# A transformer block with a written order: 75 of 168 transfers, and some instructions of three engines, change places

## The chip, the cores and the metric

The kernel runs on one core of one Trainium2 chip. The metric is the device time of one execution in microseconds (us). Before the change it is 240.98 us, the median of three runs (239.5, 240.98 and 241.52).

The core has five engines that run side by side, each through its own list of instructions: TensorE (PE; its weight loads are shown apart as PEld), VectorE (DVE), ScalarE (ACT), GpSimd (POOL) and SyncE (SP), which here only issues DMA transfers.

## The reference

One transformer block with conditioned layer norms, for 2048 tokens of 512 channels, all in bfloat16:

```python
mod = silu(c) @ w_mod                      # six vectors of 512: sa, ca, ga, sb, cb, gb
h   = layernorm(x) * (1 + ca) + sa
q, k, v = split(h @ wqkv)                  # 32 heads of 16 channels
# each token sees 8 positions: itself and 2, 4, ... 14 tokens back; earlier than 0 is masked
attn = softmax(sum_d q * k[pos - 2w] / 4)
o    = sum_w attn * v[pos - 2w]
x   = x + ga * (o @ wo)
h   = layernorm(x) * (1 + cb) + sb
x   = x + gb * ((silu(h @ w1) * (h @ w3)) @ w2)     # 1792 hidden channels
```

## The kernel before

**Tiles and stages.** The tokens are 16 tiles of 128. The first norm and the q, k and v projections go over the groups of tiles 0-1, 2-3, 4-7, 8-11 and 12-15; attention goes over pairs of tiles; the second norm and the feed-forward part (FFN) go over the groups 0-1, 2-3, 4-7, 8-11, 12-13 and 14-15. The FFN of early tiles runs on TensorE while VectorE and the DMA engines work on the attention of later ones. Names below: tile T, line Lxxx of the kernel, and the tile name that the profile shows.

- *Projections*: L691 makes q and k, four matmuls to a group, L711 makes v (`sb_v`), which SyncE stores to `v_scratch_dram`.
- *Logits of a tile*: one VectorE product q times shifted k (L742, `sb_pq`, 128x4096), summed over the channels of a head by small matmuls on TensorE (L752). These use 32-column parts of the array and are called "tiled" here, as are those of L855; all others use the whole array.
- *Softmax of a pair*: VectorE L764, L769, L794, L796, L797 (`sb_attn`) with the exponential on ScalarE (L782). TensorE turns the result over (L807), ScalarE copies it (L811, `sb_al`).
- *Values of a tile*: four DMA loads fetch the eight shifted copies of v from `v_scratch_dram` into `sb_vsh` or `sb_vshx`. VectorE multiplies them by `sb_al` (L827, 128x4096), TensorE sums them (L855), ScalarE copies the sum out of PSUM (L861, `sb_ac`), a DMA transpose makes `sb_ot`.
- *Output projection of a tile*: TensorE L867, four matmuls; VectorE L871 adds x and sums the row.
- *Second norm of a pair*: GpSimd L586 (mean), ScalarE L590 (squares, one for each tile), GpSimd L596, L597, L599 (variance, its power -0.5, bias), ScalarE L601 (normalized tile `sb_xn`, one for each tile). Then a DMA transpose into `sb_h` for each tile, and ScalarE L621 (scale and shift, four to a group); the FFN groups of tiles 0-1 and 2-3 go over TensorE and L644 instead.
- *FFN of a group*: for each of 14 blocks of 128 hidden channels, two groups of four matmuls (L883, with w1 and w3), silu on ScalarE (L889, `sb_sg`), product on VectorE (L892, `sb_hh`); then for each tile two halves of seven matmuls with w2 (L921; for tiles 14 and 15 in column halves, L909), the last addition on VectorE (L931, `sb_o`) and the store.
- *Weights* come in by loads that SyncE issues: w1, w3 and w2 in four parts each (`sb_w`). VectorE folds the gates ga and gb into wo and w2 (L946, L952).

**What sets the order.** The program is first recorded in the order of the code, each operation with what it reads and writes, and numbered (1118 operations). Nothing is planned when it is built. A table, ORDER, lists all the numbers in one sequence; each engine gets its own operations in that sequence and executes them strictly in that order, so an instruction that waits holds up everything behind it on its engine. All DMAs but one are issued by SyncE, 168 of them, in that order too. A second table, SLOTS, gives each value that lives in a pool its buffer: the eight PSUM banks, the buffers for `sb_vsh`, `sb_xn`, `sb_sg`, `sb_hh` and so on. Waits come out of both tables (place and synchronize): an operation waits for what wrote its inputs, and for everybody who used its buffer before it.

```python
for v in o.vals:
    if v.pool is not None and v.pool.last.get(v.slot) is not v:
        before = v.pool.last.get(v.slot)
        if before is not None:
            o.prev.extend(before.users)
        v.pool.last[v.slot] = v
...
for d, true in list(o.deps.items()) + [(d, False) for d in o.prev]:
    if d.dma:
        need[("dma", d.group[0].n)] = d
    elif d.eng != e or (true and e not in ("pe", "sp")):
        ...
```

So a wait on another engine is for one instruction of it, the last that is needed, and a wait on a DMA is for its whole group (the four value loads of a tile are one).

Of the kernel before, what the change touches and what calls it, by code (L numbers as in the profile page):

```python
# [272 lines left out]
def _build(p, A_x, A_wqkv, A_wo, B_w1, B_w3, B_w2, c, w_mod, out):  # L273
# [707 lines left out]
    8, 9, 10, 0, 20, 21, 22, 3, 4, 1, 2, 16, 17, 23, 24, 25, 26, 27, 28, 29, 30, 31, 32, 34, 33, 18, 59, 60, 61, 62, 63, 64, 11,  # L981
    12, 13, 65, 55, 19, 56, 5, 36, 6, 7, 57, 58, 66, 67, 68, 69, 70, 71, 72, 73, 74, 75, 76, 77, 78, 79, 80, 81, 82, 91, 38, 92,
    93, 94, 96, 97, 98, 99, 95, 101, 35, 14, 105, 83, 100, 84, 42, 40, 85, 102, 106, 86, 103, 104, 87, 39, 89, 88, 15, 141, 124,
    119, 120, 143, 142, 144, 145, 90, 146, 147, 148, 107, 173, 171, 174, 108, 172, 109, 110, 111, 181, 179, 114, 115, 175, 176,
    116, 125, 126, 127, 128, 129, 130, 182, 121, 153, 180, 154, 156, 155, 112, 177, 150, 178, 149, 152, 151, 117, 135, 131, 132,
    133, 134, 229, 122, 123, 136, 137, 113, 183, 184, 185, 138, 186, 163, 164, 237, 161, 235, 165, 238, 139, 236, 187, 193, 140,
    166, 227, 228, 189, 239, 194, 195, 188, 41, 196, 197, 198, 190, 167, 331, 230, 332, 159, 287, 168, 240, 241, 242, 231, 232,
    233, 246, 333, 289, 157, 191, 192, 211, 118, 209, 288, 234, 244, 290, 199, 162, 339, 281, 158, 160, 347, 245, 212, 210, 243,
    203, 205, 200, 215, 216, 204, 349, 169, 348, 350, 279, 340, 218, 334, 280, 351, 206, 219, 282, 352, 353, 381, 341, 372, 291,
    292, 293, 342, 207, 294, 221, 354, 355, 250, 249, 362, 247, 369, 224, 213, 336, 248, 359, 361, 214, 201, 360, 257, 258, 283,  # L990
    284, 285, 202, 371, 356, 370, 357, 358, 253, 254, 208, 273, 276, 286, 259, 260, 170, 265, 266, 217, 261, 379, 298, 380, 363,
    364, 222, 277, 365, 220, 382, 373, 374, 43, 37, 375, 295, 255, 274, 263, 297, 296, 267, 223, 256, 264, 301, 411, 413, 270,
# [12 lines left out]
    717, 700, 701, 718, 720, 509, 770, 771, 679, 705, 750, 736, 737, 490, 748, 772, 485, 719, 500, 749, 488, 721, 739, 740, 752,
    741, 507, 766, 767, 769, 489, 779, 768, 751, 754, 753, 486, 501, 773, 774, 778, 775, 776, 780, 777, 781, 782, 491, 785, 758,
    759, 760, 327, 783, 755, 529, 502, 510, 508, 492, 784, 798, 818, 511, 512, 503, 531, 532, 680, 830, 493, 513, 330, 530, 831,
    521, 539, 832, 514, 515, 820, 822, 814, 799, 815, 522, 819, 504, 505, 516, 517, 541, 494, 324, 520, 495, 518, 506, 834, 806,
    786, 807, 496, 761, 836, 794, 833, 823, 835, 677, 821, 838, 858, 808, 859, 681, 533, 534, 559, 519, 523, 535, 809, 837, 540,
    558, 542, 543, 524, 860, 525, 570, 790, 796, 795, 788, 797, 545, 861, 791, 810, 787, 789, 802, 792, 793, 526, 544, 536, 547,  # L1010
    546, 549, 548, 862, 537, 569, 538, 550, 803, 527, 528, 839, 863, 864, 804, 805, 811, 551, 594, 812, 813, 866, 824, 825, 867,
    800, 567, 593, 552, 553, 554, 874, 592, 868, 869, 826, 557, 816, 560, 801, 840, 827, 870, 871, 555, 872, 568, 556, 817, 876,
    841, 865, 854, 875, 561, 873, 846, 877, 828, 571, 842, 595, 881, 562, 572, 829, 577, 563, 584, 855, 879, 578, 579, 564, 573,
    850, 856, 580, 574, 878, 880, 906, 908, 581, 596, 565, 566, 575, 576, 954, 857, 585, 907, 583, 909, 918, 919, 894, 582, 586,
    843, 956, 955, 957, 886, 887, 958, 756, 898, 587, 588, 895, 597, 890, 891, 589, 926, 847, 598, 599, 959, 960, 962, 899, 900,
    901, 927, 961, 848, 590, 910, 600, 591, 601, 1032, 920, 921, 963, 964, 965, 892, 893, 967, 966, 1034, 928, 1033, 1035, 1036,
# [60 lines left out]
```

## Time and profile before

| | |
|---|---|
| median of three runs | 240.98 us |
| the profiled execution's own time | 239.43 us |
| its span (first to last instruction shown) | 237.7 us |
| TensorE busy | 229.7 us, 97% of the span, 1781 matmuls |
| weight loads (beside matmuls) | 136.2 us, 57% |
| VectorE busy | 179.4 us, 75% |
| ScalarE busy | 138.5 us, 58% |
| GpSimd busy | 29.2 us, 12% |
| SyncE's DMA queue (q1), share of the 16 DMA engines' time | 66.9%, 38.56 MB |
| granted TensorE clock | 1.00 |

Times in the rows are microseconds from the start of the span. A row of the timeline gives the start, the duration, the engine, the line, the operation, output and inputs, shapes, how many instructions are taken together (x4), and in brackets how long the engine had been idle before and what ended that. A row of the chain gives start, length and what the end of the program hung on in that time. The shares are means over stages of different kinds: up to about 150 us attention and FFN run side by side, and VectorE and DMA are busy; behind that only FFN is left, and VectorE and ScalarE are half idle.

### The profile page before, as it was taken

To read this page: it belongs to the slowest core of one execution; us is meant where nothing else is said; L and a number is where in the kernel's file an instruction comes from. 1 tells how busy PE (TensorE), PEld (TensorE's weight loads), DVE (VectorE), ACT (ScalarE), POOL (GpSimd) and SP (SyncE) were. 2 spreads that over 40 slices of the span, in tenths; PEclk is the share of its full clock that TensorE was granted. 3 is DMA by queue.
4 is the path that set the end of the run, shared out by engine and by line. 5 is a ranking of instruction groups with operands and counts; after the bars stand their busy time and mean duration, and the time that the engine had idled before them with its cause. 6 is when DMAs were issued, how large, how long until landed. Compare 5 with 4: busy or idle time off the path is not lost.

```text
span 237.7 us, 4535 instructions
## 1 busy us (share of the span) xinstructions
PE 229.7 (97%) x1781; PEld 136.2 (57%) x1806; DVE 179.4 (75%) x279; ACT 138.5 (58%) x267; POOL 29.2 (12%) x66
## 2 busy tenths in 40 slices
PE   7999999999999998999999999999999999999995
PEld 4776454445588674664444444444475457485774
DVE  5699999999999989999999999682654403434433
ACT  2289577999978744985865594837473405040300
POOL 4434100013002000240002520012010000000000
PEclk9999999999999999999999999999999999999999
DMA  6999999999999999897981693642203000000202
GB/s 216 372 337 322 158 237 299 208 269 283 353 200 270 243 249 199 173 260 177 247 234 47 182 234 72 154 132 46 67 19 91 3 0 0 6 19 0 70 0 88
DMA packets 46317, 38.85 MB, mean 163 GB/s; under 512 B 21704, under 2 KB 37080, under 8 KB 46296
## 3 DMA queue, kind: packets, MB, share of 16 engines
q1 hardware_dynamic: 46288, 38.56, 66.9%
q8 instruction: 14, 0.23, 0.4%
q14 instruction: 7, 0.06, 0.1%
q10 hardware_dynamic: 8, 0.00, 0.0%
HBM read 29.62 MB, written 4.21 MB: 142 GB/s over the span
## 4 chain that ended last, share of the span: by engine, by line
PE 74%; DMA 8%; DVE 8%; SPq 4%; ACT 3%; issue 2%; ACTq 0%; DVEq 0%
PE pall L883 38%; PE pall L921 18%; DMA sb_x<-in_A_x_dram 5%; PE pall L867 5%; SPq L124 4%; PE pall L691 4%; DMA sb_vsh<-v_scratch_dram 3%; PE pall L909 3%; PE pall L855 2%; PE pall L752 2%; PE pall L711 2%; DVE sb_vsh L827 2%; DVE sb_pq L742 2%; DVE sb_hh L892 1%; ACT sb_h L621 1%
## 5 line engine op out<-in xcount | busy, mean ns | idle before, releaser
L883 PE MATMUL pall<-sb_h,sb_w 128*128 128x256 bf16 (+1 forms) x664 | 101.9, 307 | 1.8 <-DVE sb_hh L892 0.9
L883 PEld LDWEIGHTS pall<-sb_h,sb_w 128*128 128x128 bf16 x672 | 64.8, 98 | 37.2 <-issue 2.8
L889 ACT ACTIVATE sb_sg<-pall 128x256 bf16<-128x256 f32 (+1 forms) x84 | 35.6, 453 | 54.1 <-PE pall L883 53.0
L892 DVE TENSOR_TENSOR sb_hh<-sb_sg,pall 128x256 bf16<-128x256 bf16 (+1 forms) x84 | 39.9, 505 | 34.8 <-PE pall L883 32.7
L921 PE MATMUL pall<-sb_w,sb_hh 128*128 128x512 bf16 x190 | 44.0, 379 | 0.3
L742 DVE TENSOR_TENSOR sb_pq<-sb_q,sb_kT 128x4096 bf16<-128x4096 bf16 x16 | 36.3, 2282 | 0.0
L921 PEld LDWEIGHTS pall<-sb_w,sb_hh 128*128 128x128 bf16 x196 | 19.0, 98 | 21.6 <-DVE sb_hh L892 0.4
L691 PE MATMUL pall<-sb_h,sb_wqkv 128*128 128x512 bf16 (+1 forms) x154 | 30.2, 335 | 0.5 <-issue 0.2
L827 DVE TENSOR_TENSOR sb_vsh<-sb_vsh,sb_al 128x4096 bf16<-128x4096 bf16 x12 | 27.3, 2287 | 2.1 <-DMA sb_vsh<-v_scratch_dram 2.1
L621 ACT ACTIVATE sb_h<-sb_h,sb_modc 128x512 bf16<-128x512 bf16 (+1 forms) x24 | 16.5, 743 | 10.1 <-DMA sb_h<-sb_xn 10.1
L691 PEld LDWEIGHTS pall<-sb_h,sb_wqkv 128*128 128x128 bf16 x160 | 14.7, 98 | 11.8 <-ACT sb_ac L861 0.4
L931 DVE TENSOR_TENSOR sb_o<-pall,sb_x 128x512 bf16<-128x512 f32 (+1 forms) x18 | 11.1, 625 | 10.5 <-PE pall L921 6.8
L711 PE MATMUL pall<-sb_wqkv,sb_h 128*128 128x512 bf16 x62 | 15.5, 379 | 0.2
L867 PE MATMUL pall<-sb_wo,sb_ot 128*128 128x512 bf16 x61 | 15.3, 379 | 0.3 <-issue 0.2
L586 POOL TENSOR_SCALAR sb_nm<-sb_sx 128x2 f32<-128x2 f32 x8 | 1.7, 218 | 105.2 <-DVE sb_x L871 105.1
L644 ACT ACTIVATE sb_h<-pall,sb_modc 128x256 bf16<-128x256 bf16 (+1 forms) x18 | 9.9, 612 | 7.5 <-DVE sb_modc L509 6.5
L861 ACT ACTIVATE sb_ac<-pall 128x512 bf16<-128x512 f32 x16 | 9.5, 595 | 7.2 <-PE pall L855 7.1
L601 ACT ACTIVATE sb_xn<-sb_x,sb_nb,sb_rs 128x512 bf16<-128x512 bf16 x16 | 12.4, 806 | 0.7 <-POOL sb_nb L599 0.6
L871 DVE SCALAR_TENSOR_TENSOR sb_x<-pall,sb_x 128x512 bf16<-128x512 f32 x16 | 10.9, 686 | 1.5 <-PE pall L867 1.3
L590 ACT ACTIVATE sb_xn<-sb_x,sb_nm 128x512 bf16<-128x512 bf16 x16 | 11.4, 714 | 0.7 <-POOL sb_nm L586 0.7
L721 ACT ACTIVATE sb_v<-pall 128x512 bf16<-128x512 f32 x16 | 9.5, 600 | 2.8 <-PE pall L711 2.8
L555 DVE BATCH_NORM_STATS2 sb_st<-sb_x 128x6 f32<-128x512 bf16 x16 | 10.6, 680 | 0.8 <-DMA sb_x<-in_A_x_dram 0.7
(87 smaller groups left out, 208.3 us busy)
## 6 DMA issues: line engine op xcount, KB each, us to landing
sb_vsh<-v_scratch_dram SPq DMA_DIRECT2D x48, 256.0 KB, 5.5
sb_vshx<-v_scratch_dram SPq DMA_DIRECT2D x16, 256.0 KB, 4.6
sb_w<-in_B_w_dram SPq DMA_DIRECT2D x6, 512.0 KB, 7.9
sb_w<-in_B_w_dram SPq DMA_DIRECT2D x6, 384.0 KB, 5.4
v_scratch_dram<-sb_v SPq DMA_DIRECT2D x16, 128.0 KB, 6.4
out_dram<-sb_o SPq DMA_DIRECT2D x14, 128.0 KB, 1.8
sb_wqkv<-in_A_wqkv_dram SPq DMA_DIRECT2D x6, 256.0 KB, 6.3
sb_x<-in_A_x_dram SPq DMA_DIRECT2D x4, 256.0 KB, 6.4
```

Source lines behind the costliest of these rows:

```text
L590: p.op("act", lambda e, vn=vn, T=T: e.activation(vn.at[:], x_sb[:, T, :], ACT.Square, bias=nm[:, T, :], accum_out=var[:, T, :]), c_act(512 ...
L601: p.op("act", lambda e, vn=vn, T=T: e.activation(vn.at[:], x_sb[:, T, :], ACT.Identity, bias=nb[:, T, :], scale=rs[:, NT + T, :]), c_act(5 ...
L621: return e.activation(vh.at[:, ft, 0:n * P], vh.at[:, ft, 0:n * P], ACT.Identity, bias=modc[:, 8 * which + ft:8 * which + ft + 1], scale=m ...
L691: ins = e.matmul(bank(vp)[:, j * n:(j + 1) * n], wqkv[:, t, col:col + P], vh.at[:, t, 0:n], start=(t == ORDER[0] and j == 0), stop=(t == O ...
L711: ins = e.matmul(bank(vp), vh.at[:, t, tt * P:(tt + 1) * P], wqkv[:, t, 2 * D:3 * D], start=(t == ORDER[0]), stop=(t == ORDER[-1]))
L742: return e.tensor_tensor(vp.at[:], in0, in1, ALU.mult)
L827: return e.tensor_tensor(v_w, v_w, a_w, ALU.mult)
L867: ins = e.matmul(bank(vy), vt.at[:, ft, :], wo[:, ft, :], start=(ft == 0), stop=(ft == KT - 1))
L883: ins = e.matmul(bank(vp)[:, 0:n], wt[:, t, fi * P:(fi + 1) * P], vh.at[:, t, 0:n], start=(t == 0), stop=(t == KT - 1))
L889: p.op("act", lambda e: e.activation(vt.at[:, 0:n], bank(vgp)[:, 0:n], ACT.Silu), c_act(n), k, r=[vgp], w=[vt], table="silu")
L892: p.op("dve", lambda e: e.tensor_tensor(vh_.at[:, 0:n], vt.at[:, 0:n], bank(vup)[:, 0:n], ALU.mult), c_dve(n), k, r=[vt, vup], w=[vh_])
L921: ins = e.matmul(bank(vz), vhh[fi].at[:, tt * P:(tt + 1) * P], w2[:, fi, :], start=(fi == 0), stop=(fi == NF - 1))
```

## The change

Only the two tables change. The operations, their shapes and their numbers are the same; so are the opening of ORDER (up to about 28 us in the trace of before) and all of GpSimd's order. Place by place, 75 of SyncE's 168 transfers and 22 to 31 operations each of TensorE (of 384), VectorE (of 263) and ScalarE (of 241) change places; counted against the longest sequence that the two orders have in common it is 69, 30, 21 and 26. SLOTS is new from the first value behind the opening on, since buffers are handed on in another sequence.

An extract of the diff; the numbers are operations:

```diff
 ORDER = [
...
-    284, 285, 202, 371, 356, 370, 357, 358, 253, 254, 208, 273, 276, 286, 259, 260, 170, 265, 266, 217, 261, 379, 298, 380, 363,
-    364, 222, 277, 365, 220, 382, 373, 374, 43, 37, 375, 295, 255, 274, 263, 297, 296, 267, 223, 256, 264, 301, 411, 413, 270,
+    359, 357, 358, 253, 371, 254, 208, 370, 286, 273, 276, 259, 297, 220, 260, 265, 266, 261, 379, 170, 296, 380, 363, 364, 222, 37,
+    277, 365, 43, 382, 255, 274, 373, 374, 375, 263, 267, 256, 264, 411, 413, 270, 298, 295, 301, 278, 49, 268, 335, 412, 262, 300,
...
-    521, 539, 832, 514, 515, 820, 822, 814, 799, 815, 522, 819, 504, 505, 516, 517, 541, 494, 324, 520, 495, 518, 506, 834, 806,
-    786, 807, 496, 761, 836, 794, 833, 823, 835, 677, 821, 838, 858, 808, 859, 681, 533, 534, 559, 519, 523, 535, 809, 837, 540,
-    558, 542, 543, 524, 860, 525, 570, 790, 796, 795, 788, 797, 545, 861, 791, 810, 787, 789, 802, 792, 793, 526, 544, 536, 547,
-    546, 549, 548, 862, 537, 569, 538, 550, 803, 527, 528, 839, 863, 864, 804, 805, 811, 551, 594, 812, 813, 866, 824, 825, 867,
+    516, 517, 541, 518, 504, 505, 506, 494, 495, 520, 834, 806, 786, 807, 496, 836, 794, 833, 593, 823, 531, 835, 821, 838, 858,
+    808, 859, 860, 861, 522, 862, 863, 864, 677, 533, 324, 534, 535, 865, 519, 523, 809, 595, 837, 540, 560, 542, 543, 524, 525,
+    790, 796, 795, 788, 797, 545, 791, 810, 557, 787, 789, 802, 792, 793, 544, 594, 547, 546, 536, 549, 548, 550, 803, 570, 761,
+    839, 804, 805, 811, 551, 812, 526, 527, 528, 537, 538, 568, 813, 866, 824, 558, 825, 867, 800, 552, 553, 554, 868, 869, 826,
...
 ]
 SLOTS = [
...
```

Where single operations went (place in ORDER before, then after):

| operations | what they are | before | after |
|---|---|---|---|
| 374 | TensorE: sum of the values of tile 1 (L855) | 301 | 306 |
| 255 | TensorE: a group of L691 | 306 | 303 |
| 391, 392, 393, 394 | SyncE: the four value loads of tile 2 | 395, 377, 391, 389 | 333, 371, 358, 345 |
| 401, 404 | SyncE: the first value loads of tile 3 | 363, 349 | 370, 365 |
| 226 | SyncE: store of v, tile 7 | 435 | 397 |
| 44, 45, 46, 47 | SyncE: loads of w3 part 0, w1 and w3 part 1, w1 part 2 | 342, 418, 426, 464 | 379, 387, 402, 407 |
| 50, 51, 52 | SyncE: loads of w3 part 3, w2 parts 0 and 1 | 448, 437, 434 | 378, 440, 411 |
| 453, 517 | TensorE: L807 of tiles 6 and 10 | 488, 709 | 492, 706 |
| 768, 769, 776, 777 | ScalarE: L601 of tiles 4, 5, 6, 7 | 651, 648, 661, 663 | 636, 633, 654, 656 |
| 859, 860 | ScalarE: L590 of tiles 8 and 9 | 733, 748 | 731, 732 |
| 861, 862, 863 | GpSimd: L596, L597, L599 of tiles 8 and 9 | 757, 772, 781 | 733, 735, 736 |
| 864, 865 | ScalarE: L601 of tiles 8 and 9 | 782, 820 | 737, 743 |
| 535, 525 | ScalarE: copies of the sums of tiles 11 and 10 (L861) | 740, 749 | 742, 754 |
| 847 | TensorE: the second L921 half of tile 5 | 886 | 851 |
| 565, 575 | TensorE: output projections of tiles 12 and 13 (L867) | 854, 856 | 864, 867 |
| 566, 576 | VectorE: their residuals (L871) | 855, 857 | 865, 868 |
| 960, 961 | ScalarE: L601 of tiles 12 and 13 | 890, 896 | 876, 875 |
| 887 | ScalarE: a silu (L889) of the FFN of tiles 8 to 11 | 874 | 880 |

In the new ORDER, then, the four value loads of tile 2 start ahead of several stores of v and weight loads; ScalarE runs both L590 and the first L601 of tiles 8 and 9 ahead of the copy of tile 11 (before, that L601 stood some 40 places behind it); and the output projections of tiles 12 and 13 stand behind one more half of L921 and two more groups of L883. At the very end the last column halves of L921 and L909 with their stores are in another sequence.

115 rows, old and new, of tables (ORDER, SLOTS) are left out of this document.

## The prediction

> **What bounds the kernel now.** I read the table by stage first, then the chain that ended last, then the timeline where a wait stands. The table's columns are the stretch, its length, the busy time of TensorE (PE), its weight loads (PEld), VectorE (DVE), ScalarE (ACT) and GpSimd (POOL), the granted clock, the share of the DMA engines, GB/s.
>
> ```profile
> core 0: us, PE busy (x) PEld busy (x) DVE busy (x) ACT busy (x) POOL busy (x), PEclk, DMA share, GB/s
> 27.00:64.00 37.00, 36.33 (x341) 18.32 (x335) 36.41 (x42) 33.07 (x62) 3.84 (x6) 1.00 1.06 264
> 64.00:88.00 24.00, 23.89 (x233) 18.42 (x236) 22.32 (x33) 18.05 (x40) 1.31 (x4) 1.00 1.12 246
> 88.00:100.00 12.00, 10.72 (x79) 5.97 (x79) 11.86 (x21) 7.49 (x14) 0.62 (x4) 1.00 0.94 186
> 100.00:127.00 27.00, 26.68 (x186) 13.90 (x189) 26.81 (x30) 17.93 (x31) 3.50 (x7) 1.00 0.87 211
> ...
> 174.00:235.00 61.00, 60.74 (x414) 40.66 (x416) 23.33 (x49) 17.30 (x41) 1.06 (x3) 1.00 0.09 27
> ```
>
> TensorE is full at clock 1.00, except at 88 to 100, where 1.28 us are missing. VectorE is as full up to 127, the DMA engines up to 88. Full could still mean slow, so the pace is checked in the chain (start, us, what), with two of its other links:
>
> ```profile
> 52.65 7.64 DMA sb_vsh<-v_scratch_dram
> 60.31 2.29 DVE sb_vsh L827
> ...
> 137.05 6.04 PE pall L883 x28
> ```
>
> 28 matmuls of 512 columns in 6.04 us are 0.216 us each, and the other long links run at that pace. So the work of TensorE, which the change leaves as it is, is a floor. A new order can gain only the few waits that are there, and it loses wherever TensorE comes to stand. One L867, L883 or L711 group of four such matmuls is 0.86 us, one half of L921 (seven) 1.51 us.
>
> **The change part by part.** Times below are on the clock of this trace; a shift that all engines share is added at the end.
>
> **1. The value loads of tiles 2 and 3 come earlier.** These are the SyncE issues around them (48.92 and 50.10 are stores of v; the other issues up to 53.29 are loads):
>
> ```profile
> 44.59 0.57 SPq L124 DMA_DIRECT2D v_scratch_dram<-sb_v  x1
> 45.20 1.20 SPq L124 DMA_TRANSPOSE sb_ot<-sb_ac  x1
> 46.45 0.59 SPq L124 DMA_DIRECT2D sb_vsh<-v_scratch_dram  x1
> 47.08 0.59 SPq L124 DMA_DIRECT2D sb_w<-in_B_w_dram  x1
> ...
> 87.14 2.29 DVE L827 TENSOR_TENSOR sb_vsh<-sb_vsh,sb_al 128x4096 bf16<-128x4096 bf16 x1 [1.04 <-DMA sb_vsh<-v_scratch_dram]
> ...
> 89.82 0.77 PEld L883 LDWEIGHTS pall<-sb_h,sb_w 128*128 128x128 bf16 x8 [1.15 <-DVE sb_hh L892]
> ```
>
> In the new order the second sb_ot transpose follows the first with no store between. It waits for the copy of tile 1, which TensorE now makes one L691 group later, so it is issued at about 44.1 and the first load at 45.3, not 46.45. The store of v11 and a 512 KB weight load no longer stand among the eight loads. The engines' share is 1.06 to 1.12, so the transfers are served one behind the other, and those up to the values of tile 7 are nearly the same set. What starts 1.1 us sooner ends about 1.1 us sooner, if the queue never runs dry. SyncE stands from about 54 to 57.7 for the copy of v7 at its new place, but some eight transfers of 256 to 512 KB are then outstanding; at 246 GB/s one takes 1.07 us or more, so they last. The 1.04 us before the product at 87.14 goes. TensorE's wait at 89.82 came from the L892 groups behind that product, so it goes as well. What is late next is the value load of tile 6, which lands just behind that of tile 7 and shifts with it. From there VectorE and TensorE are both sooner by **1.0 us**. Ends: 0 (the queue runs dry) and 1.3 (the 0.25 us between 60.06 and 60.31, where the chain hangs on the load, counted too).
>
> **2. Small moves.** The rows: TensorE behind a tiled stretch, TensorE at 64, a copy on ScalarE and its reader.
>
> ```profile
> 162.41 1.41 PEld L883 LDWEIGHTS pall<-sb_h,sb_w 128*128 128x128 bf16 x8 [0.42 <-issue]
> ...
> 63.94 0.82 PE L883 MATMUL pall<-sb_h,sb_w 128*128 128x256 bf16 x6 [0.23 <-DVE sb_attn L797]
> ...
> 104.18 0.60 ACT L811 ACTIVATE sb_al<-pall 128x512 bf16<-128x512 bf16 x1 [0.41 <-PE pall L807]
> ...
> 107.49 2.28 DVE L827 TENSOR_TENSOR sb_vshx<-sb_vshx,sb_al 128x4096 bf16<-128x4096 bf16 x1
> ```
>
> Tile 1's sum (L855) is parted from the L752 group: 15 stretches of tiled matmuls for 14, at 0.42 us each by the first row. Half of it is covered at 64, where TensorE waited 0.23 for VectorE anyway. The transposes of attention of tiles 6 and 10 (L807) move ahead of a group, to where L797 ends just then: 0.05 to 0.15 us each. Sum **+0.3 us**, ends 0 and 0.8. The reorder of L601 for tiles 4 to 7 puts ScalarE's L811 of 104.18 up to 2.5 us later; it ended at 104.78 and its reader on VectorE starts at 107.49, 2.7 later, so I take 0. The new order of the weight loads costs 0 too: the one whose lead shrinks most, the second part of w3, should land near 63 and is read at 68.5.
>
> **3. ScalarE: L601 of tile 8 ahead of the copy of tile 11.**
>
> ```profile
> 125.39 2.29 DVE L827 TENSOR_TENSOR sb_vshx<-sb_vshx,sb_al 128x4096 bf16<-128x4096 bf16 x1
> 127.59 1.28 DVE L892 TENSOR_TENSOR sb_hh<-sb_sg,pall 128x512 bf16<-128x512 bf16 x2
> 128.79 2.28 DVE L742 TENSOR_TENSOR sb_pq<-sb_q,sb_kT 128x4096 bf16<-128x4096 bf16 x1
> 131.59 2.28 DVE L742 TENSOR_TENSOR sb_pq<-sb_q,sb_kT 128x4096 bf16<-128x4096 bf16 x1
> ...
> 124.22 0.73 ACT L590 ACTIVATE sb_xn<-sb_x,sb_nm 128x512 bf16<-128x512 bf16 x1
> 127.65 0.60 ACT L861 ACTIVATE sb_ac<-pall 128x512 bf16<-128x512 f32 x1 [2.60 <-PE pall L855]
> 128.14 0.71 ACT L590 ACTIVATE sb_xn<-sb_x,sb_nm 128x512 bf16<-128x512 bf16 x1
> 129.00 0.60 ACT L861 ACTIVATE sb_ac<-pall 128x512 bf16<-128x512 f32 x1
> ...
> 129.03 2.10 POOL L596 TENSOR_SCALAR sb_rs<-sb_var 128x2 f32<-128x2 f32 x1 [6.64 <-ACT sb_xn L590]
> 131.21 0.70 POOL L597 TENSOR_TENSOR sb_rs<-sb_rs,sb_cst 128x2 f32<-128x2 f32 x1
> 131.99 1.94 POOL L599 TENSOR_TENSOR sb_nb<-sb_nm,sb_rs 128x2 f32<-128x2 f32 x1
> ...
> 129.10 3.19 PE L883 MATMUL pall<-sb_h,sb_w 128*128 128x512 bf16 x14 [0.16 <-ACT sb_xn L590]
> ```
>
> Now the copies of tiles 11 and 10 (L861) go out at 127.65 and 129.00, and the matmul at 129.10 writes into the bank that the first of them frees. In the new order ScalarE has both L590 first (124.22, 124.95), then L601 of tile 8, then that copy. L601 needs GpSimd's L596, L597 and L599. L596 would start at 125.70, in the middle of the L827 at 125.39, and the trace shows that it doesn't get through: at 129.03 it took 2.10 us and ended 0.06 after the L742 of 128.79. So: L596 ends 127.74, L597 127.82 to 128.52, L599 128.60 to 128.80, L601 starts at 128.87. ScalarE's next instruction starts 0.70 later: the copy runs 129.57 to 130.17, and the matmul of 129.10 starts at about 130.3. All behind it on ScalarE waits too: the other L601, the copy of tile 10, three L889. Their readers on TensorE follow 0.9 us apart and find them done. **+1.2 us**, which nothing later gives back on an engine that is full. Ends: 0 and +3.5; the first if L596 is through before 125.39, the second if L599 (128.60) comes to lie behind L742 (128.79) and waits 2.3 us more, as L599 did at 131.99.
>
> **4. The output projections of tiles 12 and 13 later, with L601 ahead of L889.**
>
> ```profile
> 156.57 0.69 DVE L871 SCALAR_TENSOR_TENSOR sb_x<-pall,sb_x 128x512 bf16<-128x512 f32 x1
> 157.36 0.22 POOL L586 TENSOR_SCALAR sb_nm<-sb_sx 128x2 f32<-128x2 f32 x1 [15.43 <-DVE sb_x L871]
> 159.52 1.55 POOL L596 TENSOR_SCALAR sb_rs<-sb_var 128x2 f32<-128x2 f32 x1 [1.94 <-ACT sb_xn L590]
> 166.12 0.83 ACT L601 ACTIVATE sb_xn<-sb_x,sb_nb,sb_rs 128x512 bf16<-128x512 bf16 x1
> 166.63 2.58 SPq L124 DMA_TRANSPOSE sb_h<-sb_xn  x2
> 170.40 2.07 ACT L621 ACTIVATE sb_h<-sb_h,sb_modc 128x256 bf16<-128x256 bf16 x4 [3.46 <-DMA sb_h<-sb_xn]
> 173.00 3.04 PEld L883 LDWEIGHTS pall<-sb_h,sb_w 128*128 128x128 bf16 x27
> ```
>
> TensorE does one L921 half and two L883 groups ahead of these L867: 1.51 + 2 x 0.86 = 3.2 us. The L871 of tile 13 moves from 156.57 to about 159.8, ends 160.5, and VectorE goes straight into L827 of tile 14 (160.4 to 162.7). GpSimd's L586, which took 0.22 at 157.36, meets it as L596 met one at 159.52 (1.55 us, to its end): done 162.7. Then two L590 (1.4), L596 to L599 (1.2), two L601 (1.5) end at 167.1, against 166.95 now: what ScalarE no longer queues ahead of them pays for the late start. Two transposes (2.6) and their landing (1.2) give 170.9; L621 now stands behind one more L889, and ends at 173.2 instead of 172.47. The first L883 of the group of tiles 12 and 13, that of 173.00, must wait for it until 173.3. TensorE wants them sooner than now: two L867 (1.72) have gone behind them and one L883 group (0.86) ahead, so at 172.15. **+1.1 us.** Ends: 0 (L586 gets in before L827, 2.1 us sooner) and +1.9 (the last L889 is late as well). Behind it the L867 of tiles 14 and 15 run about 12 us later, but their L883 come at 209, 20 us on: 0.
>
> **5. The end.** The last four L921 groups are permuted, not shortened; the last store hangs on the last of them as before: 0, at most +0.3.
>
> Sum: -1.0 + 0.3 + 1.2 + 1.1 = **+1.6 us**. The profiled execution took 239.43 us, 237.7 of it span; it becomes 241.0, or 0.7% more. That execution is 1.55 below the median of 240.98 (239.5 to 241.52), so on the median's scale I say **242.6**.
>
> **The rivals.**
> *A, clearly slower: GpSimd loses at 128.6.* One mechanism: the third small GpSimd instruction starts 0.19 us before L742 in my sum; if it starts after, it waits for the whole L742, and ScalarE and TensorE with it. +2.3, so +3.9: 244.9. For it: 0.19 us is less than the scatter of these steps. Against it:
>
> ```profile
> 100.75 0.20 POOL L599 TENSOR_TENSOR sb_nb<-sb_nm,sb_rs 128x2 f32<-128x2 f32 x1
> 100.83 2.28 DVE L742 TENSOR_TENSOR sb_pq<-sb_q,sb_kT 128x4096 bf16<-128x4096 bf16 x1
> ```
>
> With a start 0.08 before L742, L599 took its plain 0.20. The Trainium skill says so too ("SBUF — State Buffer", Who interferes with whom): a two-input VectorE instruction and a GpSimd read share a port pair, and whoever issues first has it for the whole instruction. By that rule the 0.19 us decide alone, and A would be out; the trace agrees here, but by the rule L742 would also have lost 0.12 us at 100.83, and its 2.28 is that of all L742.
>
> *B, the lead of part 1 is lost.* SyncE stands three times between 54 and 64.4 (v7, copies of tiles 3 and 2); if the DMA engines run dry there, the values of tile 7 land at 87.1 as now: +2.6, 243.6.
>
> *C, not slower: GpSimd first.* The same shared order, the other way: if L590 of tile 9 is done 0.3 us sooner than 125.66 relative to L827, L596 is through before it, and L601 costs 0.4 instead of 1.2; if L586 gets in ahead of the L827 of tile 14, part 4 is 0. -1.0 + 0.3 + 0.4 = -0.3: 240.7.
>
> **How the numbers follow.** Forecast 0.46 (241.5 to 244.0), A 0.20 (to 246), B 0.12, C 0.18 (down to 239.7, with part 1 at its better end), and 0.04 for something unseen, such as a weight load too late. About 1% (2.4 us) is what a measurement of this kernel tells from no change. Slower by more than that: A, half of B, the top of the forecast and the unseen, 0.37. Faster: the tail of C, 0.03. The range runs from the end of C to that of A: 239.8 to 246.0.
>
> **What would show it.** Part 1: no idle time of VectorE before L827 near 86, and TensorE 1 us ahead at 93. Part 3: ScalarE idle some 3 us before an L601 near 128, and an idle time of TensorE's L883 put down to L861. Part 4: a POOL L586 of about 2 us near 162, and L883 waiting for L621 near 172. The prediction is wrong if TensorE's busy time from 125 to 135 is as full as now, or if idle time appears in stages where I put none.

## The result and the profile after

Over 18 runs each, the changed kernel takes 242.74 us (median; 241.38 to 245.99) and the one before 239.87 (238.44 to 242.93). The ratio is **1.0144, 95% interval 1.0120 to 1.0167**: slower, by 2.9 us by the medians and 3.4 by the ratio. Executions slower than the fastest of the same kernel by over 1.5% are left out of the ratio, but not of the medians and ranges. The forecast was 242.6, and the time lies inside its range, with slower by over 1% at 0.37. That the number was hit so closely is luck: two errors cancel. The time before, taken from three runs as 240.98, is 1.1 lower by 18 runs, and the change costs about twice the +1.6 us of the sum.

The profiled execution of the changed kernel took 242.68 us, 240.9 of it span, against 239.43 and 237.7. Its table by stage, with the columns of the one shown of before (stretch, length, busy time of TensorE, weight loads, VectorE, ScalarE, GpSimd, clock, DMA share, GB/s):

```profile
64.00:88.00 24.00, 24.00 (x250) 17.96 (x243) 23.36 (x34) 18.39 (x40) 1.31 (x4) 1.00 1.14 251
88.00:100.00 12.00, 11.26 (x84) 6.29 (x83) 11.37 (x19) 7.89 (x16) 0.41 (x2) 1.00 0.90 201
100.00:127.00 27.00, 26.94 (x189) 14.25 (x187) 26.81 (x32) 18.54 (x33) 2.82 (x8) 1.00 0.77 198
174.00:235.00 61.00, 60.47 (x405) 39.41 (x404) 22.46 (x49) 19.92 (x48) 1.31 (x4) 1.00 0.10 22
```

TensorE misses less between 88 and 100 than before (0.74 us for 1.28), so something was gained there; but a stretch by the clock holds other work in each kernel. So I compared when TensorE has the same amount of work behind it in both traces, after minus before (where both orders have done the same operations, this is the start of the same one):

| at (us, before) | 24 | 84 | 93 | 96 | 109 | 127 | 132 | 144 | 150 | 168 | 174 | 234 |
|---|---|---|---|---|---|---|---|---|---|---|---|---|
| after minus before | +1.01 | +0.98 | -0.16 | +0.62 | +0.59 | +0.72 | +1.85 | +1.98 | +1.98 | +2.56 | +3.27 | +3.27 |

It starts 1.0 behind in the opening, where both orders are the same; gains 1.1 by 93 and loses 0.8 of it at 95; loses 1.1 near 130, and 1.3 between 150 and 174. Nothing changes behind. The opening is not the change's doing: both orders are the same there, and from the second load on (the first weights of the conditioning, 7.70 us for 6.71) the loads land about 1.0 us later in this execution. VectorE's wait for a load of x shows it, before and then after:

```profile
12.46 0.69 DVE L555 BATCH_NORM_STATS2 sb_st<-sb_x 128x6 f32<-128x512 bf16 x1 [0.71 <-DMA sb_x<-in_A_x_dram]
```

```profile
13.45 1.29 DVE L555 BATCH_NORM_STATS2 sb_st<-sb_x 128x6 f32<-128x512 bf16 x2 [0.94 <-DMA sb_x<-in_A_x_dram]
```

In the 13 other traces of this study (two of them with another warm-up) TensorE is 0.1 to 3.2 us behind the trace of before at 24 us, with the same order up to there. Now the three places, in the timeline of the changed kernel. At the front, VectorE's product of tile 7 has lost its wait, and an L867 has one:

```profile
87.00 2.28 DVE L827 TENSOR_TENSOR sb_vsh<-sb_vsh,sb_al 128x4096 bf16<-128x4096 bf16 x1
...
96.09 0.61 PE L867 MATMUL pall<-sb_wo,sb_ot 128*128 128x512 bf16 x2 [0.64 <-DMA sb_ot<-sb_ac]
```

Near 130, the chain of part 3: GpSimd, VectorE's L742, ScalarE, TensorE.

```profile
126.55 1.72 POOL L596 TENSOR_SCALAR sb_rs<-sb_var 128x2 f32<-128x2 f32 x1 [3.62 <-ACT sb_xn L590]
128.36 0.71 POOL L597 TENSOR_TENSOR sb_rs<-sb_rs,sb_cst 128x2 f32<-128x2 f32 x1
129.14 0.20 POOL L599 TENSOR_TENSOR sb_nb<-sb_nm,sb_rs 128x2 f32<-128x2 f32 x1
...
129.33 2.29 DVE L742 TENSOR_TENSOR sb_pq<-sb_q,sb_kT 128x4096 bf16<-128x4096 bf16 x1
...
129.38 0.81 ACT L601 ACTIVATE sb_xn<-sb_x,sb_nb,sb_rs 128x512 bf16<-128x512 bf16 x1 [2.90 <-POOL sb_nb L599]
130.10 0.58 ACT L861 ACTIVATE sb_ac<-pall 128x512 bf16<-128x512 f32 x1
...
130.73 1.47 PE L883 MATMUL pall<-sb_h,sb_w 128*128 128x512 bf16 x6 [1.10 <-ACT sb_ac L861]
```

Between 162 and 176, that of part 4:

```profile
161.76 0.69 DVE L871 SCALAR_TENSOR_TENSOR sb_x<-pall,sb_x 128x512 bf16<-128x512 f32 x1 [0.16 <-PE pall L867]
162.37 2.29 DVE L827 TENSOR_TENSOR sb_vsh<-sb_vsh,sb_al 128x4096 bf16<-128x4096 bf16 x1
...
162.54 2.19 POOL L586 TENSOR_SCALAR sb_nm<-sb_sx 128x2 f32<-128x2 f32 x1 [17.98 <-DVE sb_x L871]
...
164.77 0.72 ACT L590 ACTIVATE sb_xn<-sb_x,sb_nm 128x512 bf16<-128x512 bf16 x1 [5.01 <-POOL sb_nm L586]
167.67 1.52 ACT L601 ACTIVATE sb_xn<-sb_x,sb_nb,sb_rs 128x512 bf16<-128x512 bf16 x2 [1.37 <-POOL sb_nb L599]
172.99 0.60 ACT L889 ACTIVATE sb_sg<-pall 128x512 bf16<-128x512 f32 x1 [0.40 <-DVE sb_hh L892]
173.48 2.07 ACT L621 ACTIVATE sb_h<-sb_h,sb_modc 128x256 bf16<-128x256 bf16 x4
...
169.72 4.86 PEld L883 LDWEIGHTS pall<-sb_h,sb_w 128*128 128x128 bf16 x24 [0.94 <-ACT sb_sg L889]
175.60 2.41 PEld L883 LDWEIGHTS pall<-sb_h,sb_w 128*128 128x128 bf16 x23 [1.02 <-ACT sb_h L621]
```

ScalarE stands idle for 5.01 us behind L586, and for 1.37 more; seven L889 and copies queue behind it, and TensorE waits twice.

### The profile page after: what moved, and what is told of

The parts are those of the page before. It is cut to its first block, busy times and chain, and to the rows that moved or that the text cites. A ratio compares the mean times of both kernels' runs of the same rounds, so it can differ in the third digit from the quotient of the medians.

```text
span 240.9 us, 4562 instructions
## 1 busy us (share of the span) xinstructions
PE 233.2 (97%) x1806; PEld 136.3 (57%) x1806; DVE 179.5 (75%) x279; ACT 138.1 (57%) x267; POOL 26.5 (11%) x66
## 4 chain that ended last, share of the span: by engine, by line
PE 67%; DMA 9%; ACT 8%; DVE 6%; POOL 4%; issue 2%; SPq 2%; ACTq 0%; DVEq 0%
PE pall L883 31%; PE pall L921 13%; PE pall L691 7%; PE pall L867 5%; DMA sb_ot<-sb_ac 5%; PE pall L711 4%; DMA sb_x<-in_A_x_dram 3%; PE pall L909 3%; DVE sb_st L555 2%; PE pall L752 2%; SPq L124 2%; ACT sb_xn L601 2%; ACT sb_h L621 2%; DVE sb_pq L742 2%; ACT sb_sg L889 2%
## 5 line engine op out<-in xcount | busy, mean ns | idle before, releaser
L883 PE MATMUL pall<-sb_h,sb_w 128*128 128x256 bf16 (+1 forms) x672 | 102.4, 308 | 2.1 <-ACT sb_ac L861 1.1
L883 PEld LDWEIGHTS pall<-sb_h,sb_w 128*128 128x128 bf16 x672 | 64.8, 98 | 38.1 <-ACT sb_ac L861 1.6
L892 DVE TENSOR_TENSOR sb_hh<-sb_sg,pall 128x256 bf16<-128x256 bf16 (+1 forms) x84 | 39.6, 506 | 32.8 <-PE pall L883 24.6
L889 ACT ACTIVATE sb_sg<-pall 128x256 bf16<-128x256 f32 (+1 forms) x84 | 35.6, 456 | 45.9 <-PE pall L883 44.4
L921 PE MATMUL pall<-sb_w,sb_hh 128*128 128x512 bf16 x196 | 44.8, 379 | 0.0
L742 DVE TENSOR_TENSOR sb_pq<-sb_q,sb_kT 128x4096 bf16<-128x4096 bf16 x16 | 36.4, 2285 | 0.0
L691 PE MATMUL pall<-sb_h,sb_wqkv 128*128 128x512 bf16 (+1 forms) x160 | 31.2, 337 | 0.4 <-DVE sb_st L555 0.4
L921 PEld LDWEIGHTS pall<-sb_w,sb_hh 128*128 128x128 bf16 x196 | 18.9, 98 | 22.1 <-issue 0.4
L827 DVE TENSOR_TENSOR sb_vsh<-sb_vsh,sb_al 128x4096 bf16<-128x4096 bf16 x13 | 29.4, 2288 | 0.1
L931 DVE TENSOR_TENSOR sb_o<-pall,sb_x 128x512 bf16<-128x512 f32 (+1 forms) x18 | 11.2, 630 | 16.2 <-PE pall L921 12.4
L691 PEld LDWEIGHTS pall<-sb_h,sb_wqkv 128*128 128x128 bf16 x160 | 14.6, 97 | 12.0 <-issue 0.9
L621 ACT ACTIVATE sb_h<-sb_h,sb_modc 128x512 bf16<-128x512 bf16 (+1 forms) x24 | 16.2, 746 | 6.2 <-DMA sb_h<-sb_xn 6.2
L590 ACT ACTIVATE sb_xn<-sb_x,sb_nm 128x512 bf16<-128x512 bf16 x16 | 11.4, 717 | 11.1 <-POOL sb_nm L586 11.1
L586 POOL TENSOR_SCALAR sb_nm<-sb_sx 128x2 f32<-128x2 f32 x8 | 3.7, 465 | 122.3 <-DVE sb_x L871 122.3
L601 ACT ACTIVATE sb_xn<-sb_x,sb_nb,sb_rs 128x512 bf16<-128x512 bf16 x16 | 12.5, 809 | 7.3 <-POOL sb_nb L599 7.1
L867 PE MATMUL pall<-sb_wo,sb_ot 128*128 128x512 bf16 x64 | 15.5, 379 | 0.6 <-DMA sb_ot<-sb_ac 0.6
L711 PE MATMUL pall<-sb_wqkv,sb_h 128*128 128x512 bf16 x64 | 16.0, 379 | 0.0
L871 DVE SCALAR_TENSOR_TENSOR sb_x<-pall,sb_x 128x512 bf16<-128x512 f32 x16 | 10.9, 685 | 3.7 <-PE pall L867 3.6
L861 ACT ACTIVATE sb_ac<-pall 128x512 bf16<-128x512 f32 x16 | 9.2, 594 | 6.1 <-PE pall L855 3.7
## 6 DMA issues: line engine op xcount, KB each, us to landing
v_scratch_dram<-sb_v SPq DMA_DIRECT2D x16, 128.0 KB, 5.0
out_dram<-sb_o SPq DMA_DIRECT2D x14, 128.0 KB, 1.8
```

Of the source, the lines that this page charges most:

```text
L601: p.op("act", lambda e, vn=vn, T=T: e.activation(vn.at[:], x_sb[:, T, :], ACT.Identity, bias=nb[:, T, :], scale=rs[:, NT + T, :]), c_act(5 ...
L621: return e.activation(vh.at[:, ft, 0:n * P], vh.at[:, ft, 0:n * P], ACT.Identity, bias=modc[:, 8 * which + ft:8 * which + ft + 1], scale=m ...
L691: ins = e.matmul(bank(vp)[:, j * n:(j + 1) * n], wqkv[:, t, col:col + P], vh.at[:, t, 0:n], start=(t == ORDER[0] and j == 0), stop=(t == O ...
L711: ins = e.matmul(bank(vp), vh.at[:, t, tt * P:(tt + 1) * P], wqkv[:, t, 2 * D:3 * D], start=(t == ORDER[0]), stop=(t == ORDER[-1]))
L742: return e.tensor_tensor(vp.at[:], in0, in1, ALU.mult)
L827: return e.tensor_tensor(v_w, v_w, a_w, ALU.mult)
```

## The experiments

ORDER can be cut: where both orders have done the same (or all but the same) operations, one can be followed up to there and the other behind, with the buffers renamed at the seam. (Compared place by place, the lists of SyncE, TensorE, VectorE and ScalarE differ in 118, 100, 51 and 76 places, since one moved operation shifts those behind it; the 75 and the 22 to 31 given ahead come from one matching of the lists.)

### One stage at a time

```diff
 # x1_front: the new order for its first 594 places (96 us), the old one behind
-ORDER = old
+ORDER = new[:594] + [n for n in old if n not in new[:594]]
 # x2_mid: old, new from place 704 to 832 (118 to 148 us), old
 # x3_tail: old[:832], then new
```

> The new order up to the second transpose group of tiles 4 to 7 (about 96 us, where both orders have done the same operations), the old order behind it: parts 1 and 2 alone. By the prediction: -1.0 + 0.3 = -0.7 us against before (ratio 0.997), VectorE without its wait of 1.04 near 87. What the trace of the changed kernel suggests instead: TensorE is 1.2 us ahead at 93, and gives 0.8 back at 95 to 96, where L867 waits for the transpose of tile 7, so -0.4 us (0.998). Rival B (lead lost): 0 (1.000), and the wait of VectorE near 87 is there.

> The old order up to about 118 us, the new one from there to about 148, the old one behind: part 3 alone. By the prediction +1.2 us (ratio 1.005): GpSimd's L596 ends with the L827 that it meets, L601 starts 3 us after its L590, and L883 waits some 1.2 us longer for the copy of tile 11. Rival A: +3.5 (1.015), L599 of 2.3 us or more. Rival C: 0 to +0.4 (1.001).

> The old order up to about 148 us, the new one behind: parts 4 and 5 alone. By the prediction +1.1 us (ratio 1.005), TensorE waiting once, at the first L883 of tiles 12 and 13. By the trace of the changed kernel two waits, 0.6 at an L883 for ScalarE's L889 and 0.7 at that first L883: +1.3 (1.0055). Rival C: 0 (1.000). If the end (part 5) costs what part 4 doesn't explain, up to +0.3 more, behind 225 us.

Measured, as ratios to before, 12 runs each against 35 of before (median 239.32):

| new order in | ratio (95%) | us |
|---|---|---|
| front | 1.0018 (0.9981 to 1.0055) | +0.4 |
| middle | 1.0051 (1.0015 to 1.0086) | +1.2 |
| tail | 1.0046 (1.0008 to 1.0084) | +1.1 |

Parts 3 and 4 cost what the prediction said. The sum is +2.7 us; the whole, 1.0144, makes +3.4 with an interval from +2.9, so that up to some half us stays without a place, within the intervals of the three. What is wrong is the front: its interval, -0.5 to +1.3 us, leaves out the gain of 0.7 that was forecast. Its trace does show the gain (TensorE 0.27 behind before at 36 us, 0.38 ahead at 109), and in its timeline VectorE has no wait ahead of L827:

```profile
86.25 2.28 DVE L827 TENSOR_TENSOR sb_vsh<-sb_vsh,sb_al 128x4096 bf16<-128x4096 bf16 x1
95.12 1.04 PE L867 MATMUL pall<-sb_wo,sb_ot 128*128 128x512 bf16 x4 [0.47 <-DMA sb_ot<-sb_ac]
```

### The front: is it the transfers, and why does an L867 wait?

```diff
 # x4_front_load: x1_front, one load of values of tile 8 (489) behind the transpose of tile 6 (462)
-... 489, ... 462, ...
+... 462, 489, ...
 # x13_sp_front: the old order on all engines but SyncE; SyncE has that of x1_front
```

> The first experiment of this set with one load of values of tile 8 issued behind the transpose of tile 6 in place of between the transposes of tiles 7 and 6. If that load, issued 0.04 us behind the transpose of tile 7, is what delays its landing by 2 us: L867 at 95 no longer waits 0.6, and the time falls by 0.6 to 0.8 us against the first experiment, to -1.0 to -1.2 against before (ratio 0.995). If the weight load issued before it is the cause: no change against the first experiment (within 0.1 us).

> Before, with SyncE's new order up to 96 us alone: the other engines keep their old orders. If the transfers are what moves the time at the front: as the first experiment, VectorE's wait near 87 gone and the ratio to before within 0.3% of it (0.999 to 1.004). The transpose of tile 7: if the order of the transfers makes it late, it lands 2.9 us behind the end of its issue here too; if the fetch of instructions does, it lands 1.1 us behind, as the fetch keeps its place among TensorE's instructions, and the time is 0.5 to 0.8 us below the first experiment (0.997).

The load of tile 8 isn't it: 1.0017 (0.9986 to 1.0048), the transpose still 2.8 us behind the end of its issue. But this trace, with the front of x1_front up to 92 us, has the wait that the change was to remove:

```profile
87.36 2.29 DVE L827 TENSOR_TENSOR sb_vsh<-sb_vsh,sb_al 128x4096 bf16<-128x4096 bf16 x1 [1.03 <-DMA sb_vsh<-v_scratch_dram]
```

And kernels with the old front have it shorter: 0.30 us in x9_silu_first (below), none in x12_before_warm.

```profile
86.41 2.29 DVE L827 TENSOR_TENSOR sb_vsh<-sb_vsh,sb_al 128x4096 bf16<-128x4096 bf16 x1 [0.30 <-DMA sb_vsh<-v_scratch_dram]
```

So the landing of these values scatters by more than the lead. In traces whose openings differ by at most 1 us, they land at 85.4 to 87.3 in the new order (six traces, mean 86.4) and at 85.4 to 87.4 in the old one (six, mean 86.7); the wait is 0, 0, 0, 0.28, 0.85 and 1.03 in the new, and 0, 0.30, 0.42, 1.04, 1.05 and 1.15 in the old. The means differ by 0.3 us, not 1.0, and that is less than the scatter of either set. Two things go with the scatter, neither of them tested. In ten of the 14 traces, of both orders, the DMA queue moves next to no data for 0.9 to 1.5 us between 67.8 and 72 us, with loads outstanding (69.2 to 70.5 in the trace of before); a 16 KB packet that fetches instructions starts 0.5 to 1.3 us before the standstill. The third of the four loads lands at 84.3 to 87.3 in these ten, and at 82.9 to 83.4 in the four others. The fourth load, which ends the wait, follows 1.0 to 1.9 us later in the ten, and 2.2 to 3.5 in the four.

x13_sp_front, SyncE's order alone, is at 1.0028 (1.0003 to 1.0053): slower by itself, by an interval that hardly clears 1. TensorE leads by 1.2 us at 90, and then loses 1.0 of it:

```profile
90.89 3.65 SPq L124 DMA_TRANSPOSE sb_ot<-sb_ac  x2
95.24 1.04 PE L867 MATMUL pall<-sb_wo,sb_ot 128*128 128x512 bf16 x4 [0.97 <-DMA sb_ot<-sb_ac]
```

The DMA view of the same trace from 91.6 to 95.6 us, in slices of 0.1 us:

```profile
GB/s 1 0 0 0 15 161 287 287 287 228 46 164 1 0 0 0 0 0 0 0 0 0 0 0 0 0 18 169 282 289 289 207 49 8 0 0 1 0 0 0
q8 instruction: 1, 0.02, 2.0%
```

The transpose of tile 7 ends its issue at 92.09 and moves its data at 92.0 to 92.7, at once, with the queue empty. Yet it counts as landed at 95.19, 3.1 us behind. What comes at 92.8, at the end of its data, is one 16 KB packet of q8, the queue that fetches instructions. Over the 14 traces, the two transposes of tiles 7 and 6 land 1.1 to 1.7 us behind the end of their issue in 19 cases, and 2.2 to 3.1 in nine; in these nine, and in none of the others, such a fetch begins between 0.25 us before and 0.91 after that end. (The bounds are read off these same 28 cases.) In the old order it falls on the transpose of tile 6 or on none (8 of 8), in the new one on that of tile 7, which TensorE wants at once (5 of 5; 0.4 to 1.0 us of wait; the sixth, with another warm-up, follows below). The packet takes about 1 us, so the time of the packet alone doesn't make the 2 us of delay. In x13_sp_front 30 of the 32 four-byte packets that close the transpose are through at 92.90; the last two end at 94.11, just as the fetch's packet does (92.79 to 94.10), and the landing follows 1.1 us later.

By its expectation, the 3.1 us of x13_sp_front speak for the order of the transfers as the cause. They don't separate the two, since the fetch had moved as well (below). What separates them is the transpose of tile 6 in the eight traces with the old order there (one of them with the other warm-up): in one and the same order of transfers it lands late in the four where the fetch falls on it, and on time in the other four.

The Trainium skill ("Runtime: NRT & Kernel Launch", Instruction fetch mechanics) has each engine's instructions refilled in blocks of 16 KiB, 256 instructions, by a DMA queue of its own, at a cost "mostly hidden". The 14 packets of q8 here fit 1806 weight loads and as many matmuls; hidden it is not, for a transfer that it meets.

### Moving the fetch

```diff
 # x11_front_warm: x1_front, x12_before_warm: the kernel before; both with
-            return e.matmul(bank(vw)[:, 0:256], ones[:, 0:P], ones[:], start=True, stop=True)
+            if i % 2 == 0:
+                return e.matmul(bank(vw), ones[:, 0:P], bass.AP(ones, 0, [[256, P], [0, 2], [1, 256]]), start=True, stop=True)
```

> The first experiment (new order up to 96 us) with the 24 warm-up matmuls of 256 columns at the start made 12 of 512: the same busy time, 24 instructions of TensorE less, so that every 16 KB fetch of instructions comes later by the time of 24 instructions (about 1.5 to 2.6 us near 93). If the transpose of tile 7 lands late (2.9 us behind the end of its issue in the first experiment, 1.1 in before) because the fetch of 92.9 falls on it: it lands 1.1 us behind again, L867 does not wait for it near 95, and the time falls by 0.5 to 0.8 us, to 0.997 of before. If it lands late because of the order of the transfers ahead of it: 2.9 us and the time of the first experiment (1.002) stay.

> The kernel before, with its 24 warm-up matmuls of 256 columns made 12 of 512 and nothing else: the control of the run with the new order up to 96 us and the same edit (ratio 0.9987). If that run gained because the fetch no longer falls on the transpose of tile 7: nothing to gain here, where it did not fall on it, ratio 1.000 (0.998 to 1.002), and the transpose lands 1.1 us behind the end of its issue as before. If the shorter warm-up is itself the gain: 0.997, 0.7 us below before, and TensorE's projections start earlier by as much near 12 us.

With 24 instructions less, the fetch of x11_front_warm comes 1.55 us behind the end of issue, the transpose lands 1.21 behind, and no L867 waits. But the edit hardly moved the fetch: it comes at 93.10, 0.23 us later than in x1_front (92.87), not the 1.5 to 2.6 that I expected, while the issue of the transpose ends 0.66 sooner (91.55 for 92.21). The time is 0.9987 of before (0.9964 to 1.0010), 0.7 us below x1_front, with intervals that overlap. But the control is 0.9970 (0.9942 to 0.9999): the edit gives as much where the fetch had harmed nothing. So the landing again goes with the distance to the fetch, but the 0.7 us can't be put down to it. Nor is the gain of the control explained: TensorE's projections start no earlier (0.24 later at 12 us than in the first trace); its profiled execution of 237.89 us is one without VectorE's wait. It is the fastest kernel of the study by median (238.50), by an interval that hardly clears 1. And what sets the time of a fetch stays open: in x13_sp_front TensorE's order is the old one, the fetch should have kept its place by my expectation, and came at 92.8, not 95.4.

### The middle: ScalarE's order, and GpSimd behind L827

```diff
 # x5_act_only: the kernel before; ScalarE's 860 (L590) and 864 (L601) ahead of 535 (copy of tile 11)
-533, 534, 559, 519, 523, 535, ... 860, 525, ... 861, ... 862, ... 863, ... 864
+533, 534, 559, 519, 523, 860, 861, 862, 863, 864, 535, ... 525
 # x7_av_late: the changed kernel; two L892 ahead of the L827 of tile 10 (523)
-523, 809, ... 837
+837, 809, 523
```

> Before, with one change on ScalarE alone: the L590 of tile 9 and the L601 of tile 8 go ahead of the copy of tile 11 (L861); TensorE, VectorE, SyncE and GpSimd keep their orders. If part 3 is ScalarE's order and GpSimd's wait behind L827, as the prediction has it: +1.2 us against before (ratio 1.005), L596 of 1.5 to 2.1 us that ends with an L827, and a wait of some 1.4 us at the L883 behind the two L855 groups near 129. If it takes the other moves of that stage too: 0 (1.000).

> The changed kernel with VectorE's order alone changed near 126: two L892 go ahead of the L827 of tile 10, so that GpSimd's L596 of tiles 8 and 9 (ready at 126.5) meets an instruction that reads PSUM, or idle time, and no L827. If L596 of 1.72 us was a wait for that L827: it takes about 0.2 us, L599 ends near 127.9 and L601 of tile 8 starts at 128.0 in place of 129.4, 1.6 us after its L590. If L596 is slow for another reason: 1.7 us and 129.4 as in the changed kernel. The time is not expected to fall by the same amount (0 to -0.5 us against the changed kernel), since the L827 of tile 10 itself comes 1.9 us later, and with it the second L855 group.

x5_act_only costs 1.0047 (1.0018 to 1.0075), +1.1 us: two instructions on ScalarE make the whole of part 3. Its rows are those of the prediction:

```profile
125.89 1.91 POOL L596 TENSOR_SCALAR sb_rs<-sb_var 128x2 f32<-128x2 f32 x1 [3.44 <-ACT sb_xn L590]
...
128.90 0.81 ACT L601 ACTIVATE sb_xn<-sb_x,sb_nb,sb_rs 128x512 bf16<-128x512 bf16 x1 [3.09 <-POOL sb_nb L599]
...
130.47 0.81 PE L883 MATMUL pall<-sb_h,sb_w 128*128 128x512 bf16 x3 [1.46 <-ACT sb_ac L861]
```

In x7_av_late the L827 of tile 10 no longer runs when L596 is ready (VectorE is at an L892, which reads PSUM), and L596 takes a ninth of the time:

```profile
126.50 0.19 POOL L596 TENSOR_SCALAR sb_rs<-sb_var 128x2 f32<-128x2 f32 x1 [3.50 <-ACT sb_xn L590]
126.78 0.70 POOL L597 TENSOR_TENSOR sb_rs<-sb_rs,sb_cst 128x2 f32<-128x2 f32 x1
127.56 0.19 POOL L599 TENSOR_TENSOR sb_nb<-sb_nm,sb_rs 128x2 f32<-128x2 f32 x1
...
127.79 0.82 ACT L601 ACTIVATE sb_xn<-sb_x,sb_nb,sb_rs 128x512 bf16<-128x512 bf16 x1 [1.37 <-POOL sb_nb L599]
...
130.71 0.61 PE L855 MATMUL pall<-sb_vsh,sb_ind 128*32 128x512 bf16 x8 [1.56 <-DVE sb_vsh L827]
```

L601 starts at 127.79, expected 128.0. The time was not expected to fall much, and it did not fall: 1.0167 (1.0136 to 1.0197, four runs) of before, for 1.0144 of the changed kernel. TensorE now waits 1.56 for the L827 that came later. The delay was only moved.

### The tail: which of the moves costs?

```diff
 # x8_wo_back: x3_tail; L867 and L871 of tiles 12, 13 and an L921 half in the old places
-906, 847, 848, 908, ... 918, 894, 565, 566, 575, 576, ... 926
+906, 908, 565, 575, 566, 576, 918, 894, ... 926, 847, 848
 # x9_silu_first: x3_tail; ScalarE's list
-956, 955, 961, 960, 887, 895, 588, 598
+887, 956, 955, 895, 588, 598, 961, 960
 # x10_av14_first: x3_tail; VectorE's list (596 and 586: L827 of tiles 15 and 14; 848: L931)
-848, 596, 909, 566, 576, 586
+596, 848, 909, 586, 566, 576
```

> The third experiment (the new order behind 148 us), with the L867 of tiles 12 and 13, their L871 and the L921 half of tile 5 back in their old places; ScalarE keeps the new order (L601 ahead of L889). If the late output projections are the cause of part 4: the cost of the third experiment, 1.1 us, is gone (ratio 1.000 against before, 1.1 below the third). If ScalarE's order is the cause: it stays (1.0046).

> The third experiment, with ScalarE's L889 and copies put among the norm's instructions of tiles 12 and 13 (one L889 ahead of L590, one L889 and two copies between L590 and L601). The wait of 0.6 at an L883 near 169 goes. If the norm's chain L586 to L621 alone sets the price, the wait at the first L883 of tiles 12 and 13 grows by as much and the time stays within 0.3 us of the third experiment (ratio to before 1.004 to 1.006). If the two waits add up, it is 0.6 us faster than the third (1.002).

> The third experiment, with VectorE's order alone changed near 155 to 163: the L931 of tile 5 behind the L827 of tile 15, and the L827 of tile 14 ahead of the L871 of tiles 12 and 13, so that no L742 or L827 follows the last L871. If L586 waits for that L827: it takes 0.22 in place of 2.19 us, starts 0.5 us later, the norm is done about 1.5 us sooner, both waits of TensorE near 169 and 175 go, and the time is about 1.1 us below the third experiment (ratio to before 1.000 to 1.001). If the late output projections set the price by themselves: as the third experiment (1.0046) or above.

**x10_av14_first**: 0.9990 (0.9953 to 1.0028), the cost of the tail is gone, with the output projections as late as in x3_tail. L586 takes its 0.22, and TensorE runs through, but for 0.20 at a weight load:

```profile
162.97 0.22 POOL L586 TENSOR_SCALAR sb_nm<-sb_sx 128x2 f32<-128x2 f32 x1 [19.24 <-DVE sb_x L871]
...
167.04 6.79 PEld L883 LDWEIGHTS pall<-sb_h,sb_w 128*128 128x128 bf16 x32
174.02 5.68 PEld L883 LDWEIGHTS pall<-sb_h,sb_w 128*128 128x128 bf16 x48 [0.20 <-ACT sb_h L621]
```

**x9_silu_first**: 1.0014 (0.9980 to 1.0047), about 0.8 us below x3_tail, with intervals that overlap; in its trace the tail costs 0.67 us, in that of x3_tail 1.43. By the traces my theory, that the norm's chain alone sets the price, falls: the first wait is gone and the second has not grown.

```profile
168.23 0.60 ACT L889 ACTIVATE sb_sg<-pall 128x512 bf16<-128x512 f32 x1 [0.41 <-PE pall L883]
170.04 2.07 ACT L621 ACTIVATE sb_h<-sb_h,sb_modc 128x256 bf16<-128x256 bf16 x4 [1.21 <-DMA sb_h<-sb_xn]
```

Here L621 waits for its transposes. In the changed kernel it followed at once on an L889 that ended at 173.59, which had itself waited for an L892 (rows of 172.99 and 173.48 above): the queue that formed on ScalarE behind L586 came back to it through VectorE.

**x8_wo_back**: 1.0102 (1.0064 to 1.0140), 1.3 us above x3_tail, as neither theory had it. L586 is free (0.22), the norm's L601 are done at 163.9, in x3_tail at 167.6, and two other waits have come with the edit: L867 is early again, but its transpose stands behind a store and a load of values in SyncE's new order; and an L883 waits for the L931 that I had put back without its neighbours.

```profile
158.53 0.22 POOL L586 TENSOR_SCALAR sb_nm<-sb_sx 128x2 f32<-128x2 f32 x1 [16.72 <-DVE sb_x L871]
...
156.67 1.04 PE L867 MATMUL pall<-sb_wo,sb_ot 128*128 128x512 bf16 x4 [1.02 <-DMA sb_ot<-sb_ac]
170.75 2.55 PE L883 MATMUL pall<-sb_h,sb_w 128*128 128x512 bf16 x11 [1.38 <-DVE sb_o L931]
```

It says nothing on the price of the late L867; x10_av14_first does.

## Why the prediction was right, and where not

- **The frame** (work of TensorE as a floor, every change a wait gained or lost) held: the difference of both traces is five steps in TensorE's starts, and between them the two run in parallel within 0.3 us.
- **Part 1, -1.0: the term that failed.** Its mechanism is there: VectorE's wait goes and TensorE gains 1.1 us by 93. The step "what starts 1.1 us sooner ends about 1.1 us sooner" doesn't hold from one execution to the next: in the same order the values land anywhere in 2 us, and the wait of 1.04 that I took from one profile is between 0 and 1.15 in others of the same front. A difference of 0.3 in the means is left, within the scatter. The cost that I didn't have is the transpose of tile 7, 0.4 to 1.0 us at an L867; I had looked for what is late next among the value loads (tile 6, rightly no trouble), not among the transposes behind them. By the sign that I had set, idle time in a stage where I put none, the prediction of the front is wrong. Front together: +0.4 measured for -0.7 forecast, nearly the whole gap between +1.6 and +2.9. Rival B (lead lost) had the outcome of the front right, but the loss comes at the transpose near 95, not at the values of tile 7. Its condition, a queue that runs dry, is left open: the queue does stand still between 67.8 and 72 us in ten traces of both orders, and no run tests what that costs.
- **Part 2, +0.3**: nothing to be seen (+1.01 at 24 us, +0.98 at 84), at its lower end. That the wait at an L883 of 63.94 before and the extra tiled stretch cancel is my reading, not shown alone.
- **Part 3, +1.2**: right in mechanism and size (+1.1 in the trace of the changed kernel, 1.0051 and 1.0047 in the two that have it alone). Rival A did not come: L599 started 0.19 us ahead of L742, just the margin of the sum. By the rule of the Trainium skill that the prediction cites, the earlier one gets the port; this trace agrees (L599 took its plain 0.20), but is a weak test, since the two overlap by 0.01 us.
- **Part 4, +1.1**: right in size (1.0046), in part by luck, and right in its origin, L586 behind L827 (2.19 us, foreseen as about 2). The step "must wait for it until 173.3" has the second wait only. In the trace of x3_tail it costs 0.69, not 1.1. The first, at L889, was the upper end of +1.9; it costs 0.74 there, and the +1.1 had nothing for it. L621 was held by ScalarE's queue rather than by its own late transposes.
- **Part 5, 0**: right, +3.27 at 174 and at 234 us.
- **The scale**: three runs gave a median 1.1 us above that of 18; with the base of 239.87 the same sum would have said 241.5, and 242.74 would have been near the upper end of the forecast's own range, 240.4 to 242.9.

## What to carry to other kernels

In a kernel that one engine fills, price a new order by its waits, one by one, and ask of each wait in a profile whether it is there in every execution: one that hangs on a DMA landing may be a matter of chance, while one that hangs on another engine's order came back within about 0.2 us here (L586 behind L827 2.19 us in four traces, L596 1.72 to 1.93 in three). Small instructions of GpSimd on the path to a busy engine belong where VectorE has no long two-input instruction; an in-order queue behind them (ScalarE here) turns 2 us of theirs into waits in several places. An edit that puts back a few instructions without what they used to wait for makes new waits, so undo a whole stage, or one engine's list.

## What the runs showed that I had not expected

Where a 16 KB instruction fetch begins close to the end of a DMA transpose's issue, the transpose lands 2.2 to 3.1 us behind that end, not 1.1 to 1.7 (nine cases of nine, against 19 without). And the same transfers in the same order land up to 2 us apart from one execution to the next, near 87 us, which is more than the difference between the two kernels' fronts (+0.4 us by the runs). The runs of one kernel spread over more still (before: 237.85 to 241.70 in 35 runs).
